# Block-sorted attention and an MLP on one core: more opening matmuls, instruction fetches in the planner, and K and V of three batches sorted on the whole array

## The chip, the cores and the metric

The kernel runs on one core of one Trainium2 chip. A core has five engines that run side by side: PE (TensorE, matrix multiplication, into the accumulators called PSUM), DVE (VectorE), ACT (ScalarE), POOL (GpSimd) and SP (SyncE, which here only issues DMAs). Each works through its own list of instructions in order, and they wait for each other by semaphores. DMA moves data between the chip's main memory and the on-chip memory (SBUF, 128 partitions). The metric is the device time of one execution in microseconds (us), lower is better; the time before is the median of three runs.

## The reference

Attention over blocks that are first mixed by a learned, normalised matrix, and then a two-layer MLP with a leaky activation. There are 4 batches, 8 heads, 768 rows of 64; 8 blocks of 96 rows per head.

```python
P = sort_net                                  # 4 x 8 x 8 x 8
for _ in range(5):
    P = P - np.max(P, axis=-1, keepdims=True)
    P = np.exp(P)
    P = P / (np.sum(P, axis=-1, keepdims=True) + 1e-09)
    P = P / (np.sum(P, axis=-2, keepdims=True) + 1e-09)
k_sorted = np.einsum('bhij,bhjcd->bhicd', P, k_b)      # k, v as 8 blocks of 96 rows
v_sorted = np.einsum('bhij,bhjcd->bhicd', P, v_b)
scores = scale * np.matmul(q_b, k_sb.transpose(0, 1, 2, 4, 3))   # inside each block
attn = softmax(scores)
x = np.matmul(attn, v_sb)                     # then to 3072 tokens x 512
h = x @ w_in                                  # 512 x 2048
g = np.maximum(h, 0.0) + alpha * np.minimum(h, 0.0)
out = g @ w_out                               # 2048 x 512
```

"Sorting" below is the product with P over the blocks.

## The kernel before

**A plan written out ahead.** The kernel first builds a graph of operations. Each operation (`G.add`) names its engine or engines, the instructions it issues, an estimated duration, what it reads and writes, and a priority (smaller is earlier). `schedule` fills all engines by list scheduling with these durations, `span` gives one operation's begin and end, `replay` runs the found order again with random extra durations, and `search` repeats the whole 1500 times with slightly changed priorities and keeps the order with the smallest end. `emit` then writes the order of each engine into the program, with semaphore waits. So the order on every engine is fixed before the kernel runs, and a change of an estimated duration changes the order. `fill` puts warm-up matmuls (L883) into gaps of PE up to the start of the MLP.

**Inputs.** POOL issues the loads of q, k, v and the weights, which are converted from float32 to bfloat16 on the way. q, k and v of a batch come as 128 partitions of 3072 elements (`load_q`, `load_kv`); a partition holds half a block, 48 rows. Later batches' loads are paced: they wait for a certain transpose of the attention (`paced`), so that they do not crowd out the transposes.

**Sort matrices.** `sinkhorn` makes P on DVE and ACT for all batches. `spread` widens it with small PE matmuls and builds on DVE one matrix per batch, `BDK`, of 128 x 128 with one 8 x 8 block per head and half; batch 0 at once, batches 1 to 3 after the first x tile is written.

**Sorting.** K of a batch is sorted in 6 units, V in 8 (`prep_k`, `prep_v`). A K unit is 16 matmuls of 64 x 64 (L540, in `pairs`): 8 columns groups, each as an upper and a lower half of the array. A V unit is 16 matmuls of 128 x 64 weights (L583), which write the upper and lower half of the output. V is first copied from its staging tile `VST` into `VD`, where each group of 48 columns is widened to 64 (`conv_v`); for batches 1 to 3 POOL does this, in 8 copies for each batch. `VD` holds a whole batch. The sorted units go from PSUM to `KT` and `VS` by ACT or DVE.

**Attention.** `attention(g)` runs for 32 groups (4 batches of 8 blocks): scores (L618, L621), the maximum on DVE (L627), exponentials on ACT (L654, L665), the product with V (L674), division on DVE (L681, L684). In batch 0 the scores are made a second time in transposed form (L633, L642), and the result is turned on PE (L699); in later batches SP issues DMA transposes of the exponentials (`ET<-Esb`) and of the result (`xT<-xq`).

**MLP.** `ffn1` (L721) multiplies tiles of x by `w_in`, ACT and DVE apply the activation (L731, L734) into `hT`, and `ffn2` (L760) multiplies by `w_out`. It runs in pieces of 2 or 4 groups, interleaved with the attention of later groups.

**The opening.** 70 small matmuls (`burst`, L785) keep PE busy from the start. Then come q's reordering (L540 on `QS`), the sort network, K and V of batch 0, two groups of attention and the first MLP step. Loads in order of issue on POOL: q, k, v of batch 0, `w_in` in four pieces of 512 columns, `w_out` in two, k of batch 1, q of batch 1, then v of batch 1 and k, v of batch 2.

Of the kernel before, what the change touches and what calls it, by code (L numbers as in the profile page):

```python
# [25 lines left out]
NE = 3  # L26
EPS = 1e-9
SEARCH = 1500

# [18 lines left out]
class _Op:  # L48
    __slots__ = ("eng", "fn", "dur", "prio", "deps", "dma", "idx", "pos", "inc", "start", "end",
                 "users", "left", "ready", "turn", "engs", "base")  # L50

    def __init__(self, eng, fn, dur, prio, dma, idx):
        self.eng, self.fn, self.dur, self.prio, self.dma, self.idx = eng, fn, dur, prio, dma, idx
        self.deps = set()
        self.turn = set()
        self.users = []
        self.inc = None
        self.engs = eng


class _Graph:
# [7 lines left out]
    def add(self, eng, fn, dur, r=(), w=(), prio=0.0, dma=None):  # L69
        op = _Op(eng, fn, dur, prio, dma, len(self.ops))  # L70
        if eng == ("pool",) and dma is None:
            w = list(w) + ["pool cores"]
# [19 lines left out]
    def span(self, op, e, at, free, loads, more=0.0):  # L92

        if op.dma is None:
            d = op.dur[e] if isinstance(op.dur, dict) else op.dur
            return at + d * (1 + more), at + d * (1 + more)
# [7 lines left out]
        return at + 1300, loads[1]  # L104

# [13 lines left out]
    def schedule(self):  # L119
# [17 lines left out]
        loads = [0.0, 0.0]  # L137
# [30 lines left out]
    def replay(self, seed):  # L168
# [5 lines left out]
        loads = [0.0, 0.0]  # L174
# [3 lines left out]
        last = max(op.end for op in self.ops)  # L178
        for op, (a, b) in zip(self.ops, was):
            op.start, op.end = a, b  # L180
        return last

    def search(self, n):
# [4 lines left out]
        for x in range(n):  # L188
            amp = rng.choice((0.1, 0.3, 1.0))
            for op, p in zip(self.ops, rank):  # L190
                op.prio = p + (rng.uniform(-amp, amp) if x and p > -47.5 and rng.random() < 0.1 else 0.0)
            cost = self.schedule()
            if best is None or cost < best + 1500:
                cost = (cost + self.replay(1) + self.replay(2)) / 3
# [95 lines left out]
def bass_sinkhorn_attn__then__act_prelu_kernel(  # L290
# [38 lines left out]
    dsel = sb("dsel", [128, 3, 8], F32)  # L329
    BDK = sb("BDK", [128, 4, 128], BF16)  # L330
    epst = sb("epst", [32, 8], F32)
# [7 lines left out]
    QS = [sb("QS0", [128, 3072], BF16)]  # L339
# [3 lines left out]
    VD = sb("VD", [128, 64, 64], BF16)  # L343
# [3 lines left out]
    Es0 = [sb("Es0%d" % n, [112, 800], BF16) for n in range(2)]  # L347
# [8 lines left out]
    outstg = [sb("outstg%d" % n, [128, DM], F32) for n in range(4)]  # L356
    dtmp = outstg[3]

# [28 lines left out]
    d_v = [dma_sem("v%d" % n) for n in range(7)]  # L387
# [8 lines left out]
    def load_q(b, prio):  # L396
        if b == 0:
            G.add(POOL, lambda e: e.dma_start(QS[0][:, :], AP(q.tensor, 0, [[3072, 128], [1, 3072]])),
# [30 lines left out]
    def load_v(b, prio):  # L429
        load_kv(VST, v, "VST", d_v, 9, b, prio)  # L430

    def consts():
# [7 lines left out]
        G.add(POOL, lambda e: e.memset(AP(VD, 48, [[4096, 128], [64, 64], [1, 16]]), 0.0), 900,  # L440
              w=["VD0"], prio=-95.5)
        for n in range(2):
            G.add(DVE, lambda e, n=n: e.memset(AP(Es0[n], 768, [[800, 112], [1, 32]]), 0.0), 100, w=[("Es0p", n)], prio=-88)
        for n in range(NE):
            G.add(DVE, lambda e, n=n: e.memset(AP(ET[n], 768, [[800, 128], [1, 32]]), 0.0), 100, w=[("ETp", n)], prio=-30)
# [13 lines left out]
        for n in range(NE):  # L459
# [4 lines left out]
              r=["identf"], w=["mkj"], prio=-70)  # L464
        G.add(DVE, lambda e: e.tensor_reduce(one0[:, :], AP(identf, 0, [[128, 112], [64, 2], [1, 48]]),
# [13 lines left out]
    def bc(t):  # L479
        return AP(t, 0, [[8, 32], [1, 8], [0, 8]])  # L480

# [25 lines left out]
    def spread(bs, prio):  # L507
        n = len(bs)

        def f(e):  # L510
# [4 lines left out]
        G.add(PE, f, 100 * n, r=["Pb", "selk"] + [("xT", 1)] * (bs[0] > 0), w=PSP, prio=prio)  # L515
        G.add(DVE, lambda e: e.tensor_tensor(
            out=AP(dtmp, 0, [[512, 128], [8, 8 * n], [1, 8]]),
            in0=AP(psYP, 512, [[1024, 128], [8, 8 * n], [1, 8]]),
            in1=AP(mkj, 0, [[8, 128], [0, 8 * n], [1, 8]]), op=AluOpType.mult), 150 + 70 * n,
            r=PSP + ["mkj"], w=["dtmp", ("out", 3)], prio=prio)  # L520
        G.add(DVE, lambda e: e.reduce_sum(AP(dsel, 0, [[24, 128], [1, 8 * n]]),
                                          AP(dtmp, 0, [[512, 128], [8, 8 * n], [1, 8]]),
                                          axis=AxisListType.X), 150 + 70 * n,
              r=["dtmp", ("out", 3)], w=["dsel"], prio=prio)
        for x, b in enumerate(bs):
            G.add(DVE, lambda e, x=x, b=b: e.tensor_tensor(
                out=AP(BDK, b * 128, [[512, 128], [16, 8], [2, 8], [1, 2]]),
                in0=AP(mkh, 0, [[16, 128], [2, 8], [0, 8], [1, 2]]),
                in1=AP(dsel, x * 8, [[24, 128], [0, 8], [1, 8], [0, 2]]), op=AluOpType.mult), 260,
                r=["dsel", "mkh"], w=[("BDK", b)], prio=prio)  # L530

    def pairs(src, n, u, mat, off_m, row_m, bank):
        t, off, row, keys = bank

        def f(e):
            inst = None
            for c in range(8):
                cc = 8 * u + c
                for hp in range(2):
                    inst = e.matmul(AP(t, hp * 64 * row + off + c * 64, [[row, 64], [1, 64]]),  # L540
                                    AP(src, hp * 64 * 3072 + cc * 64, [[3072, 64], [1, 64]]),
# [4 lines left out]
    def prep_q(u, prio, bank):  # L546
        t, off, row, keys = bank
        G.add(PE, pairs(QS[0], 0, u, identb, 0, 128, bank), 372, r=[("QS", 0), "identb"], w=keys, prio=prio)
        o = AP(QTz[0], 8 * u, [[6144, 128], [96, 32], [48, 2], [1, 8]])
        i = AP(t, off, [[row, 128], [2, 32], [1, 2], [64, 8]])  # L550
        G.add(EITHER, lambda e: copy(e, o, i), t_either(512), r=keys, w=[("Q0", u)], prio=prio)
# [374 lines left out]
```

## Time and profile before

| | before |
|---|---|
| median of 3 runs | 259.07 us (257.0 to 260.28) |
| the profiled execution | 259.23 us |
| its span, first to last instruction | 257.5 us |
| mean granted PE clock | 0.973 |
| warm-up matmuls L883 | 37, 11.6 us busy |
| MLP matmuls L721 to psH | 556, 97.0 us busy |
| MLP matmuls L760 to psYP | 306, 80.0 us busy |

The profile gives, for one execution, the busy time of each engine, groups of equal instructions by source line, the waits with what ended them, and a chain of work followed back from the last instruction. PE's matmuls are pipelined: the length of one matmul (200 to 400 ns) is its way through the array, while the next begins long before. What a group of matmuls costs PE is therefore the distance between its start and the start of the next group. PEld is the loading of weights, which runs beside the matmuls. "issue" as a releaser means that the engine waited for nothing the profile shows. A few records of matmuls are missing.

### The profile page before, as it was taken

Reading aid. Unit: us, or ns where it says so; the run is one execution under the profiler, and the core shown is the slowest. Engines: PE = TensorE matmul, PEld = TensorE weight load, DVE = VectorE, ACT = ScalarE, POOL = GpSimd, SP = SyncE. Lnnn points to the kernel's source line nnn. Section 1 sums busy time; section 2 is a strip of 40 time slices with the busy share of each in tenths; the row PEclk is TensorE's granted clock in tenths of the full one; section 3 lists DMA queues with packets and bytes.
Section 4 is the critical chain, followed back from the end, with each engine's and each line's share of the span. In section 5 each row is a group of like instructions: output and inputs, shape, how many; then the busy total and the mean of one; then the engine's idle time right before and its main releaser. Section 6 shows DMA issues by size and latency. Waiting matters only on the chain.

```text
span 257.5 us, 6566 instructions
## 1 busy us (share of the span) xinstructions
PE 238.7 (93%) x2721; PEld 147.2 (57%) x2752; DVE 166.2 (65%) x330; ACT 154.1 (60%) x419; POOL 61.4 (24%) x89
## 2 busy tenths in 40 slices
PE   7687799979999997989899999999999999999995
PEld 4355577767656564645565565555555565555544
DVE  5773577666676896756887667466477795655510
ACT  4473444555775976758856654857667775555511
POOL 8999000194493020867100000000000000000000
PEclk9997779988999999999999999999999999999999
DMA  5999999999299989999985961212537234201112
GB/s 100 214 203 203 190 217 165 215 173 196 66 89 197 142 128 158 174 179 178 138 141 129 162 136 59 44 45 75 118 93 97 47 95 113 71 5 40 76 44 83
DMA packets 77070, 32.17 MB, mean 125 GB/s; under 512 B 67808, under 2 KB 73200, under 8 KB 77040
## 3 DMA queue, kind: packets, MB, share of 16 engines
q0 software_dynamic: 25168, 13.63, 40.8%
q1 hardware_dynamic: 51872, 18.11, 38.5%
q8 instruction: 21, 0.34, 0.6%
q14 instruction: 9, 0.07, 0.1%
HBM read 27.28 MB, written 6.29 MB: 130 GB/s over the span
## 4 chain that ended last, share of the span: by engine, by line
PE 76%; DMA 8%; POOL 6%; DVE 3%; issue 3%; ACT 3%; POOLq 0%
PE psH L721 28%; PE psYP L760 25%; DMA ET<-Esb 8%; PE psYP L583 4%; PE psS L760 3%; PE psO L674 3%; PE psS L618 3%; PE psS L633 2%; PE psYP L540 2%; ACT Esb L654 1%; POOL QN L447 1%; PE psYP L883 1%; POOL w_in_bf L803 1%; PE psS L642 1%; PE psO L583 1%
## 5 line engine op out<-in xcount | busy, mean ns | idle before, releaser
L734 DVE SCALAR_TENSOR_TENSOR hT<-t,omaT,psH 128x384 bf16<-128x384 f32 (+1 forms) x139 | 77.6, 572 | 41.2 <-ACT t L731 39.7
L721 PE MATMUL psH<-xT,w_in_bf 128*128 128x384 bf16 (+1 forms) x556 | 97.0, 312 | 0.9 <-DVE hT L734 0.7
L731 ACT ACTIVATE t<-psH 128x384 f32<-128x384 f32 (+1 forms) x139 | 62.3, 465 | 42.5 <-PE psH L721 39.8
L760 PE MATMUL psYP<-w_out_bf,hT 128*128 128x512 bf16 x306 | 80.0, 382 | 2.9 <-issue 1.3
L721 PEld LDWEIGHTS psH<-xT,w_in_bf 128*128 128x128 bf16 x556 | 50.9, 98 | 33.9 <-DVE hT L734 5.9
L654 ACT ACTIVATE Esb<-psS,nf 96x96 bf16<-96x96 f32 x192 | 46.3, 344 | 1.5 <-DVE nf L627 1.3
L760 PEld LDWEIGHTS psYP<-w_out_bf,hT 128*128 128x128 bf16 x336 | 30.6, 98 | 27.9 <-issue 0.6
L373 POOL COPY VD<-VST 128x384 bf16<-128x384 bf16 x26 | 22.6, 869 | 33.8 <-DMA VST<-in_v_dram 25.7
L627 DVE TENSOR_REDUCE nf<-psS 96x8 f32<-96x768 f32 x24 | 22.7, 948 | 2.1 <-PE psS L618 1.9
L684 DVE TENSOR_TENSOR xq<-psO,rec 96x512 bf16<-96x512 f32 x31 | 21.3, 687 | 1.1
L402 POOL DMA_DIRECT2D QN<-in_q_dram x24 | 19.8, 845 | 2.3 <-DMA xT<-xq 1.8
L373 ACT ACTIVATE outstg<-psYP 128x512 f32<-128x512 f32 x15 | 9.0, 597 | 12.7 <-PE psYP L760 12.7
L583 PE MATMUL psYP<-BDK,VD 128*64 128x64 bf16 x416 | 12.1, 202 | 3.5 <-issue 2.0
L681 DVE RECIPROCAL rec<-psO 96x8 f32<-96x8 f32 x31 | 6.2, 201 | 13.2 <-PE psO L674 13.1
L373 ACT ACTIVATE VS<-psYP 112x512 bf16<-112x512 f32 x14 | 9.7, 690 | 7.6 <-PE psYP L583 7.2
L583 PEld LDWEIGHTS psYP<-BDK,VD 128*64 128x64 bf16 x416 | 9.1, 114 | 8.6 <-issue 4.2
L618 PEld LDWEIGHTS psS<-KT,QTz 128*96 128x96 bf16 x192 | 11.6, 124 | 3.2 <-ACT Esb L654 0.4
L373 ACT ACTIVATE KT<-psYP 128x512 bf16<-128x512 f32 x13 | 7.8, 597 | 9.5 <-PE psYP L540 9.5
L618 PE MATMUL psS<-KT,QTz 128*96 128x96 bf16 x192 | 12.8, 209 | 0.0
L674 PEld LDWEIGHTS psO<-VS,ET 112*128 112x128 bf16 x192 | 8.6, 98 | 6.4 <-DMA ET<-Esb 3.0
L883 PE MATMUL psYP<-identb 128*128 128x512 bf16 x37 | 11.6, 438 | 0.3 <-ACT identb L373 0.3
L674 PE MATMUL psO<-VS,ET 112*128 112x65 bf16 x192 | 9.9, 194 | 1.6 <-DMA ET<-Esb 1.6
(116 smaller groups left out, 183.3 us busy)
## 6 DMA issues: line engine op xcount, KB each, us to landing
out_dram<-outstg SPq DMA_DIRECT2D x23, 256.0 KB, 2.3
KS<-in_k_dram POOLq DMA_DIRECT2D x3, 768.0 KB, 30.0
VST<-in_v_dram POOLq DMA_DIRECT2D x3, 768.0 KB, 26.7
QN<-in_q_dram POOLq DMA_DIRECT2D x24, 96.0 KB, 6.5
w_in_bf<-in_moe_w_in_dram POOLq DMA_DIRECT2D x4, 512.0 KB, 17.2
w_out_bf<-in_moe_w_out_dram POOLq DMA_DIRECT2D x2, 1024.0 KB, 27.1
QS<-in_q_dram POOLq DMA_DIRECT2D x1, 768.0 KB, 7.1
VST<-in_v_dram POOLq DMA_DIRECT2D x4, 192.0 KB, 5.4
```

The lines of the kernel that those rows point to most:

```text
L373: return e.activation(o, i, ACTF.Copy) if e is nc.scalar else e.tensor_copy(o, i)
L402: G.add(POOL, lambda e, h=h: e.dma_start(AP(QN, h * 128 + (h // 4) * 64, [[6144, 128], [1024, 6], [1, 64]]), AP(q.tensor, b * HB + h * S * ...
L583: inst = e.matmul(AP(t, th * 64 * row + off + dd * 64, [[row, 64], [1, 64]]), AP(VD, (8 * u + dd) * 64, [[4096, 128], [1, 64]]), AP(BDK, b ...
L618: inst = e.matmul(o, AP(QTz[n], hp * 3072 + h4 * 768 + i * 96, [[6144, 128], [1, 96]]), AP(KT[n], (h4 * 8 + i) * bk, [[ld, 128], [64, 2], ...
L627: G.add(DVE, lambda e: e.tensor_reduce(AP(nx, 0, [[8, 96], [4, 2], [1, 4]]), AP(psX, 0, [[1024, 96], [512, 2], [96, 4], [1, 96]]), AxisLis ...
L654: inst = e.activation(AP(Esb[me], p * 128, [[1024, 96], [64, 2], [1, 48]]), AP(psX, (p // 4) * 512 + (p % 4) * 96, [[1024, 96], [48, 2], [ ...
L674: inst = e.matmul(AP(psZ, hp * 512 + h4 * 68, [[1024, 128], [1, 65]]), AP(ET[me] if far else Es0[m], pos(h4, hp) * 96, [[800, nk], [1, 128]]),
L684: G.add(DVE, lambda e: e.tensor_tensor(out=AP(xq[me], 0, [[512, 96], [256, 2], [64, 4], [1, 64]]), in0=AP(psZ, 0, [[1024, 96], [512, 2], [ ...
L721: inst = e.matmul(AP(pt, poff, [[1024, 128], [1, n]]), AP(w_in_bf, kt * DFF + ft * 128, [[KT_TILES * DFF, 128], [1, 128]]), AP(xT, kt * XR ...
L731: G.add(ACT, lambda e: e.activation(AP(t1[tb], 0, [[384, 128], [1, n]]), AP(pt, poff, [[1024, 128], [1, n]]), ACTF.Relu, scale=-1.0), t_ac ...
L734: G.add(DVE, lambda e: e.scalar_tensor_tensor(out=AP(hT, ft * RING + tok % RING, [[FT_TILES * RING, 128], [1, n]]), in0=AP(t1[tb], 0, [[38 ...
L760: inst = e.matmul(AP(bank[0], bank[1], [[1024, 128], [1, n]]), AP(hT, ft * RING + tok % RING, [[FT_TILES * RING, 128], [1, 128]]), AP(w_ou ...
```

## The change

- The opening burst has 140 matmuls instead of 70.
- The planner gets a model of PE's instruction fetches: a count of PE's instructions, with a mark every 256, and the next mark cannot be passed earlier than 6.2 us after the last one. `search` has a first phase of 500 rounds that minimises the sum of the ends of the first four x tiles, and then the 1500 rounds of before, which now vary only priorities above 0.
- K of batches 1 to 3: POOL copies each unit in two halves into a ring of three units (`KSz`), in which each group of 64 columns lies in a field of 128 whose other half is zero. A unit is then 8 matmuls with 128 x 128 weights instead of 16 with 64 x 64. The moving operand is a new compact matrix `BDM`.
- V of batches 1 to 3: loaded as two halves (first and second halves of blocks on different partitions), copied in two halves per unit into a ring of four units (`VDz`) in the same manner; for batch 1 the second halves may go to ACT or DVE, all others go to POOL. 8 matmuls per unit, with a matrix `BDV`.
- `spread` of batches 1 to 3 makes these two matrices per batch: six more matmuls and more DVE steps; there are three more masks. POOL zeroes the two rings once.
- `w_in` comes in four pieces of 128 rows instead of 512 columns, and each MLP step reads all four.
- Batch 0's `VD` and `QS` lie in the space of `hT`; `Es0` is replaced by `ET`; q's units of batch 0 are copied by ACT alone.

```diff
+FIRST = 500
+FETCH = 6200.0
+BURST = 140
...
+            if e == "pe":
+                return (self.fetched(op, at, d * (1 + more), loads[2]),) * 2
...
+    def fetched(self, op, at, d, f):
+
+        if f["fills"] and at > 5000:
+            f["n"] += 2 * int(max(at - f["end"], 0) * 0.9 / 215)
+        f["fills"] = f["fills"] and op.fills
+        n, last = 2 * op.mm, f["n"] + 2 * op.mm
+        while f["mark"] < last:
+            x = at + d * max(f["mark"] - f["n"], 0) / n
+            late = max(f["usable"] - x, 0.0)
+            at, x = at + late, x + late
+            f["usable"] = x + FETCH
+            f["mark"] += 256
+        f["n"], f["end"] = last, at + d
+        return at + d
...
-        for x in range(n):
+        for x in range(FIRST + n):
+            if x == FIRST:
+                best = None
+            lo, hi, part = (-47.5, 3.0, 0.2) if x < FIRST else (0.0, 99.0, 0.1)
...
+            if x < FIRST:
+                cost = sum(op.end for op in first)
...
+        n = 2 if b == 3 else 1
+        t = 3072 // n
+        for x in range(2 * n):
+            G.add(POOL, lambda e, th=x % 2, c=x // 2 * t: e.dma_start(
+                AP(VST[b % 2], th * 64 * 3072 + c, [[3072, 64], [1, t]]),
+                AP(v.tensor, b * HB + th * 3072 + c, [[6144, 64], [1, t]])), load_us / (2 * n),
...
+        G.add(POOL, lambda e: e.memset(zk[:, :], 0.0), 1500, w=[("KSz", u, hp) for u in range(3) for hp in range(2)],
+              prio=0.05)
...
+    def conv_k(b, u, prio):
+        n = b % 2
+        for hp in range(2):
+            G.add(POOL, lambda e, hp=hp: e.tensor_copy(
+                AP(KSz, hp * 64 * 3072 + u % 3 * 1024 + hp * 64, [[3072, 64], [128, 8], [1, 64]]),
+                AP(KS[n], hp * 64 * 3072 + 8 * u * 64, [[3072, 64], [64, 8], [1, 64]])), 900,
+                r=[("KS", n)] + [("KS", n, x) for x in range(4)], w=[("KSz", u % 3, hp)], prio=prio)
...
+            for c in range(8):
+                inst = e.matmul(AP(t, off + c * 64, [[row, 128], [1, 64]]),
+                                AP(KSz, (u % 3 * 8 + c) * 128, [[3072, 128], [1, 128]]),
+                                AP(BDM, b * 64, [[256, 128], [1, 64]]))
...
-        G.add(POOL if b or u % 3 == 2 else EITHER, lambda e: copy(e, o, i), {"act": 858, "dve": 540, "pool": 720},
-              r=[("VST", b % 2)] + [("VST", b % 2, x) for x in range(4)], w=[("VD", u)], prio=prio)
...
+        for th in range(2):
+            o2 = AP(VDz, th * 64 * VSL * 1024 + u % VSL * 1024 + th * 64, [[VSL * 1024, 64], [128, 8], [1, 48]])
+            i2 = AP(VST[b % 2], th * 64 * 3072 + 8 * u, [[3072, 64], [1, 8], [64, 48]])
+            G.add(EITHER if b == 1 and th else POOL, lambda e, o2=o2, i2=i2: copy(e, o2, i2),
+                  {"act": 858, "dve": 540, "pool": 830}, r=vst, w=[("VDz", u % VSL, th)], prio=prio)
...
+                if b:
+                    inst = e.matmul(AP(t, off + dd * 64, [[row, 128], [1, 64]]),
+                                    AP(VDz, (u % VSL * 8 + dd) * 128, [[VSL * 1024, 128], [1, 128]]),
+                                    AP(BDV, b * 64, [[256, 128], [1, 64]]))
+                    continue
...
-        for _ in range(70):
+        for _ in range(BURST):
...
-            AP(w_in_bf, p * 512, [[KT_TILES * DFF, 128], [DFF, KT_TILES], [1, 512]]),
-            AP(moe_w_in.tensor, p * 512, [[DFF, 128], [128 * DFF, KT_TILES], [1, 512]])),
+            AP(w_in_bf, p * DFF, [[KT_TILES * DFF, 128], [1, DFF]]),
+            AP(moe_w_in.tensor, p * 128 * DFF, [[DFF, 128], [1, DFF]])),
...
-            units = [(prep_k, b + 1, u) for u in range(6)]
+            units = [(conv_k, b + 1, u) for u in range(2)]
+            for u in range(6):
+                units += [(prep_k, b + 1, u)] + [(conv_k, b + 1, u + 2)] * (u < 4)
```

More of the change, by code (lines that the diff above doesn't have):

```diff
@@ L178, in replay @@
         last = max(op.end for op in self.ops)
+        self.ends = [op.end for op in self.ops]
         for op, (a, b) in zip(self.ops, was):
@@ L181, in replay, with search @@
         return last
-    def search(self, n):
+    def search(self, n, first):
         rng = random.Random(7)
@@ L508, in spread @@
         n = len(bs)
+        late = bs[0] > 0
+        rows = n * (1 + late)
         def f(e):
@@ L521, in spread @@
[L521 to L524, printed above, removed]
+            for x in range(n * late):
+                for hf in range(2):
+                    inst = e.matmul(AP(psYP, hf * 64 * 1024 + 512 + (n + x) * 64, [[1024, 64], [1, 64]]),
+                                    AP(selk, bs[x] * 128, [[512, 32], [2, 64]]), Pb[:, :])
```

161 lines of the change are left out of this document (116 added, 45 removed).

## The prediction

> **What bounds the kernel now.** I read the page's first part, then the stretches of the span, then the chain of waits.
>
> ```profile
> span 257.5 us, 6566 instructions
> PE 238.7 (93%) x2721; PEld 147.2 (57%) x2752; DVE 166.2 (65%) x330; ACT 154.1 (60%) x419; POOL 61.4 (24%) x89
> ...
> 0.00:32.20 32.20, 24.38 (x507) 16.37 (x507) 20.01 (x66) 15.90 (x30) 23.72 (x41) 0.89 1.04 182
> 32.20:60.00 27.80, 26.02 (x397) 19.66 (x397) 19.28 (x44) 14.18 (x34) 7.55 (x9) 0.88 1.42 195
> 60.00:130.00 70.00, 64.83 (x854) 40.66 (x863) 50.32 (x91) 50.25 (x151) 30.12 (x39) 1.00 1.22 146
> 130.00:245.00 115.00, 113.69 (x912) 64.64 (x927) 75.53 (x129) 71.69 (x202) 0.00 (x0) 1.00 0.40 86
> ```
>
> A row of a stretch gives its length, the busy time and instructions of PE, PEld, DVE, ACT and POOL, then the granted clock. Two regimes: up to 32.2 us, where the first MLP matmul starts, PE serves a chain of dependent steps; after it PE is the bound, idle 1.78, 5.17 and 1.31 us in the three later stretches. So a microsecond taken from PE's work after 32.2 is worth nearly one of the end, and one taken from the opening chain too, as all later PE work starts that much earlier. From 130 us POOL does nothing, and there is little idle time to win.
>
> The chain through the opening, and PE's and DVE's own steps around it (start, length, engine, line):
>
> ```profile
> 18.82 0.38 PE psYP L583 x11
> 19.20 2.03 issue
> 21.23 0.25 PE psYP L583 x4
> 21.48 0.75 PE psYP L883 x3
> ...
> 22.57 0.91 PE psS L633 x8
> ...
> 28.26 0.54 PE psYP L883
> ...
> 39.13 0.54 PE psS L633 x8
> ...
> 1.02 2.04 PE L785 MATMUL psS<-bz 128*32 128x32 bf16 x70 [1.02 <-DVE bz L780]
> ...
> 9.48 0.67 PE L540 MATMUL psS<-identb,QS 64*64 64x64 bf16 x32
> ...
> 14.88 0.44 PE L540 MATMUL psO<-BDK,KS 64*64 64x64 bf16 x16 [0.26 <-issue]
> ...
> 16.36 0.44 PE L540 MATMUL psH<-BDK,KS 64*64 64x64 bf16 x16
> ...
> 19.94 0.93 DVE L627 TENSOR_REDUCE nm<-psH 96x8 bf16<-96x768 f32 x1
> ...
> 32.21 1.04 PE L721 MATMUL psH<-xT,w_in_bf 128*128 128x192 bf16 x8
> ```
>
> Two things stand out. In the middle of one group of sorting matmuls PE stops for 2.03 us and waits for nothing that the profile shows. And the same eight L633 matmuls take 0.91 us at 22.57 and 0.54 at 39.13. The stretches say why:
>
> ```profile
> 14.88:19.30 4.42, 3.76 (x127) 2.65 (x127) 4.16 (x7) 4.06 (x8) 4.30 (x6) 1.00 1.23 208
> ...
> 18.86:22.27 3.41, 1.38 (x23) 0.68 (x25) 2.02 (x3) 1.67 (x3) 3.41 (x5) 1.00 1.23 203
> 22.27:25.68 3.41, 3.41 (x58) 3.02 (x60) 0.69 (x1) 0.96 (x2) 3.27 (x6) 0.53 1.24 204
> 25.68:29.10 3.42, 3.42 (x77) 2.60 (x71) 1.57 (x3) 2.03 (x3) 0.00 (x0) 0.50 1.15 173
> ```
>
> From the gap of 0.26 us before 14.88, which has no releaser either, PE had run 127 matmuls and 127 weight loads, 254 instructions; it went on at 21.23, 6.35 us after that gap. I read that as PE running out of delivered instructions: some 256 per 6.3 us. And the clock is granted at half right after a stretch in which PE was busy 1.38 of 3.41 us, the one with the stop, and stays there to about 29.
>
> **The opening, part by part.** Seventy more opening matmuls are 140 more PE instructions at the front, where PE only keeps warm: the 70 of before lie between 1.02 and 3.06 us, and 140 would end near 5.1, well ahead of the q matmuls. If instructions come in blocks of 256, every boundary falls 140 instructions, that is 70 matmuls, earlier in the work. The one that fell inside the third V unit moves back into the end of the K units, 6.3 us after a boundary in the last q matmuls near 10, thus due at about 16.3, while the last K unit starts at 16.36: no wait, or one of 0.1. The next is 128 matmuls on, some 60 past the old stop, due near 22.7, where PE would arrive near 22. So of 2.03 us I take 1.6 as won, leaving 0.4 for the boundary near 22; bounds 2.0 won and 2.0 lost (a second stop of that length). Late next is the maximum of the second score group, on DVE until 20.87, well inside the won time.
>
> In the Trainium skill, "Runtime: NRT & Kernel Launch", section "Instruction fetch mechanics", instructions are refilled in blocks of 256, which agrees with the 254 counted; it also holds that the fetch is hidden behind the sequencer's own pace, and the 2.03 us speak against that. By that section of the Trainium skill the first term would be zero, and the sum below 253.0.
>
> The clock: 21.48 to 28.26 are 6.8 us of mostly PE pieces at half clock. By the L633 pair, full clock makes it 0.54/0.91 = 0.59, so 2.8 us less. The half clock need not go altogether, since the waits of this stretch leave PE partly idle anyway; bounds 0 and 2.8, taken 2.2. What else lies below full clock from 32.2 to 60, at 0.88 on average, I leave as it is.
>
> The new search that orders the work up to the first four x tiles, and q's copies on ACT alone, I cost at nothing; the sort network on DVE still covers them. w_in now has to be there whole for the first MLP matmul:
>
> ```profile
> 4.34 3.00 POOL L803 DMA_DIRECT2D w_in_bf<-in_moe_w_in_dram  x4
> ...
> DMA to landing us min/median/max: 14.3/17.2/20.4
> ```
>
> The last is issued at about 6.6 and lands by 27.0 at the latest; the first MLP matmul would come at 32.2 − 3.8 = 28.4. Cover 1.4 us, cost zero; without that cover each microsecond of lateness costs one.
>
> **The sorting matmuls.** For batches 1 to 3 each of 6 K and 8 V units has 8 full-array matmuls instead of 16 small ones: 42 units. Prices are distances between starts of neighbours on PE:
>
> ```profile
> 128.15 0.44 PE L583 MATMUL psYP<-BDK,VD 128*64 128x64 bf16 x16
> 128.52 0.56 PE L618 MATMUL psS<-KT,QTz 128*96 128x96 bf16 x8
> ...
> 134.56 0.41 PE L674 MATMUL psO<-VS,ET 112*128 112x65 bf16 x8
> 134.80 1.47 PE L721 MATMUL psH<-xT,w_in_bf 128*128 128x384 bf16 x8
> ...
> 158.62 0.44 PE L540 MATMUL psYP<-BDK,KS 64*64 64x64 bf16 x16
> 159.00 1.04 PE L760 MATMUL psYP<-w_out_bf,hT 128*128 128x512 bf16 x4
> ```
>
> A V unit holds PE 0.37 us, a K unit 0.38. L674 has nearly the new shape (8 matmuls, 112 by 128 weights, 65 columns) and holds it 0.24. Saving 0.13 × 42 = 5.5 us, all in the regime where PE is the bound; bounds 0 (PE then waits instead) and 5.9. It also takes 336 matmuls, 672 instructions, out of the stream.
>
> **What POOL gets.** The longest waits and the copies:
>
> ```profile
> L373 POOL COPY VD<-VST x26: 829/849/1199, 17.6 to 111.1; 128x384 bf16<-128x384 bf16 x26
> L563 POOL COPY KT<-KT 128x512 bf16<-128x512 bf16 x1 | 0.7, 722 | 0.0
> ...
> 81.96 0.56 POOL L420 DMA_DIRECT2D VST<-in_v_dram  x1 [3.14 <-DMA ET<-Esb]
> 90.99 1.07 POOL L420 DMA_DIRECT2D VST<-in_v_dram  x2 [8.47 <-DMA ET<-Esb]
> 95.28 0.53 POOL L420 DMA_DIRECT2D KS<-in_k_dram  x1 [3.22 <-DMA ET<-Esb]
> 100.13 0.53 POOL L420 DMA_DIRECT2D VST<-in_v_dram  x1 [4.32 <-DMA xT<-xq]
> 103.66 1.05 POOL L420 DMA_DIRECT2D KS<-in_k_dram  x2 [3.00 <-DMA ET<-Esb]
> ```
>
> A copy works on half the partitions with as many elements in each, so I take V at 0.85 us a half and K at 0.72 (nearest row 128x512; bounds 0.36, if half the partitions cost half, and 1.20, the longest copy). Per batch: 16 × 0.85 + 12 × 0.72 = 22.2 us where 8 copies took 6.8. Three batches make 46 us more at most, 6.8 less if the eight second halves of batch 1 go to ACT or DVE; three memsets of 3584 elements in all, some 5 us at the pace of the 128x512 copy, come last in priority, and from 32.2 to 60 POOL is busy 7.55 of 27.80 us. Up to 130 us POOL is busy 61 us, so there is room in sum. But before, V was copied up to a whole batch ahead; now three K units and four V units are the lead. And POOL runs in order: behind its paced loads of batch 3 stand copies of batch 2, for them PE. I charge 1.0 us of new PE idle time; bounds −2.0, since the 5.17 us idle in 60–130 could also shrink, and +15 (a rival below).
>
> Does the copying slow DVE? "GPSIMD Engine Reference" of the Trainium skill, section "Specifications", has POOL's SBUF interface shared with VectorE, against this change. The trace shows the first row beside eight POOL copies, the second without any:
>
> ```profile
> L734 DVE SCALAR_TENSOR_TENSOR hT<-t,omaT,psH 128x384 bf16<-128x384 f32 x5 | 3.0, 609 | 1.2 <-ACT t L731 1.1
> ...
> L734 DVE SCALAR_TENSOR_TENSOR hT<-t,omaT,psH 128x384 bf16<-128x384 f32 x44 | 26.4, 611 | 13.8 <-ACT t L731 13.3
> ```
>
> No slowing of the main DVE step, so the term is nothing.
>
> The rest: six more matmuls and some eight small DVE steps, each below the 0.61 us of L734, in the second spread and the masks, and up to eight copies of batch 1 on ACT or DVE, both busy under 75% from 32 to 130 us. Charged 0.5; bounds 0 and 2.0.
>
> **The sum.** The profiled execution took 259.23 us, 1.7 outside its span; the median of the three is 259.07, 0.2 below, which I neglect. 259.23 − 1.6 − 2.2 − 5.5 + 1.0 + 0.5 = 251.4 us, 3.0% less.
>
> **Rivals.**
>
> *The opening stays.* The 2.03 us stop has another cause, or falls elsewhere, and the half clock with it. For: no row names the cause, and one boundary is still due in the same stretch. Against: 254 instructions and 6.35 us fit a block well. Time: 259.23 − 5.5 + 1.5 = 255.2. The 140 matmuls would not do what they are there for. Chance 0.17. It is also the case to which the Trainium skill's sentence on the hidden fetch leads.
>
> *POOL becomes the bound around batch 2's sorting.* Between 78 and 104 us POOL waits 22.1 us in order for transposes (the five waits above) and issues 3.7 us of loads. Batch 2's 28 copies of 22.2 us now have to fit there: 48 us of 26. If the waits are not used up by the copies that stand ahead of them, 22 us are over; the V ring hides 4 units × 1.7 = 6.8, and PE stands still for 15: 251.4 − 1.0 + 15 = 265.4, slower. It decides once more than about 14 us reach PE. Against it: a wait shrinks when POOL comes to it later, and some loads can stand behind the copies. Chance 0.14.
>
> *More than forecast.* Half of the 8.3 us of PE idle from 32 to 245 goes too, because x arrives earlier and PE has fewer small groups: 251.4 − 4.1 = 247.3. Chance 0.11.
>
> **The numbers.** The forecast has 0.58, with its own range of 247.5 to 255. Measurements of this kernel can tell about 2% from no change, that is 5.2 us: faster is below 253.9, slower above 264.2. Faster: 0.49 of the forecast's 0.58, 0.11 of the third rival, 0.01 of the first; 0.61. Slower: the second rival but for 0.02, plus 0.02 for bounds adding up; 0.14. The rest is 0.25. The range, 245.5 to 260, takes in the first and third rival and leaves out most of the second and 0.03 below.
>
> **What would show it.** Right: no issue wait of 2 us before the first MLP matmul; that matmul at 28 to 29 us; granted clock 1.00 from 20 to 28; 42 groups of eight sorting matmuls that hold PE 0.24 to 0.25 us each; PE idle between 32 and 245 us near 9. Wrong: POOL copies released late and PE waiting for KSz or VDz between 75 and 130 us; sorting units that still hold PE 0.37; the first MLP matmul waiting for w_in.

## The result and the profile after

The changed kernel takes 251.78 us (median of five runs, 249.6 to 253.86), the kernel before 258.08 us in the same comparison (257.0 to 260.28). The ratio is 0.9702, 95% interval 0.963 to 0.9775: about 3% faster. The forecast was 251.4, 3.0% less. Executions more than 1.5% above the shortest of their kernel, the profiled one below among them, count in the medians but not in the ratios, so the two can differ.

The profiled execution took 253.86 us, the longest of the five, so single waits in it are not all typical; E8 below has a second profile of the same kernel. Its first part, then its stretches (length, busy time and instructions of PE, PEld, DVE, ACT and POOL, granted clock, DMA share, GB/s), cut at the first MLP matmul, which now starts at 28.60:

```profile
span 251.9 us, 6183 instructions
...
PE 234.7 (93%) x2494; PEld 146.1 (58%) x2494; DVE 170.3 (68%) x340; ACT 156.1 (62%) x423; POOL 100.0 (40%) x146
```

```profile
0.00:28.60 28.60, 23.00 (x583) 16.13 (x583) 20.26 (x67) 16.25 (x31) 26.49 (x46) 1.00 0.95 179
28.60:60.00 31.40, 29.42 (x362) 22.16 (x356) 21.95 (x53) 16.82 (x39) 11.46 (x18) 0.84 1.36 193
60.00:130.00 70.00, 63.98 (x687) 40.29 (x686) 53.49 (x96) 52.40 (x155) 56.52 (x75) 1.00 1.19 151
130.00:245.00 115.00, 114.13 (x841) 64.30 (x838) 74.22 (x127) 69.69 (x199) 5.56 (x10) 1.00 0.37 86
```

The opening is 3.6 us shorter and runs at full clock throughout. PE is idle 1.98, 6.02 and 0.87 us in the later stretches, 8.87 in all, where the forecast had "near 9". POOL has gone from 61.4 to 100.0 us. But from 28.6 to 60 the clock is 0.84 on average. Three finer stretches of the same profile show where the low clock went:

```profile
18.86:22.27 3.41, 3.22 (x88) 2.14 (x83) 2.02 (x4) 1.82 (x4) 3.17 (x6) 1.00 1.06 214
22.00:28.60 6.60, 4.87 (x101) 3.63 (x93) 4.71 (x9) 3.28 (x5) 6.60 (x10) 1.00 1.09 181
28.60:34.00 5.40, 5.40 (x59) 4.03 (x54) 3.63 (x13) 1.69 (x4) 0.50 (x1) 0.68 1.22 200
```

From 18.86 to 22.27 PE was busy 1.38 us before and is busy 3.22 now: the stop is gone. No "issue" is among the waits of PE. The half clock now comes after 28.6, in the first MLP work.

From the timeline of PE (start, length, line, matmul, count): the first MLP matmul, then a K unit and a V unit, each with the group that follows it.

```profile
28.60 0.82 PE L854 MATMUL psH<-xT,w_in_bf 128*128 128x192 bf16 x4
...
45.65 0.39 PE L664 MATMUL psYP<-BDM,KSz 128*128 128x64 bf16 x8
45.88 0.49 PE L854 MATMUL psH<-xT,w_in_bf 128*128 128x192 bf16 x4
...
135.95 0.40 PE L705 MATMUL psYP<-BDV,VDz 128*128 128x64 bf16 x8
136.18 1.47 PE L854 MATMUL psH<-xT,w_in_bf 128*128 128x384 bf16 x8
```

Each unit holds PE 0.23 us, against 0.37 and 0.38 before. POOL's copies and its longest waits (copies: count, busy us, mean ns, idle before; waits: total us, times, longest):

```profile
L423 POOL COPY VDz<-VST 64x384 bf16<-64x384 bf16 x40 | 33.7, 842 | 13.6 <-PE psYP L705 11.5
L651 POOL COPY KSz<-KS 64x512 bf16<-64x512 bf16 x36 | 22.1, 614 | 36.6 <-PE psYP L664 21.0 <-DMA KS<-in_k_dram 13.8
```

```profile
POOL QN L452 <- DMA xT<-xq: 1.7, 2, 0.9
POOL KS L470 <- DMA xT<-xq: 0.9, 1, 0.9
```

POOL's paced loads wait for transposes 2.6 us in all; before it was 25.9, of which the five waits quoted in the prediction made 22.1. The 21.0 us in the second copy row are POOL waiting for PE to give a ring slot back, so POOL has time over. And in this execution PE never waits for `KSz` or `VDz`.

### The profile page after: what moved, and what is told of

Read it like the earlier page. It is cut to its first block, busy times and chain, and to the rows that moved or that the text cites. A ratio compares the mean times of both kernels' runs of the same rounds, so it can differ in the third digit from the quotient of the medians.

```text
span 251.9 us, 6183 instructions
## 1 busy us (share of the span) xinstructions
PE 234.7 (93%) x2494; PEld 146.1 (58%) x2494; DVE 170.3 (68%) x340; ACT 156.1 (62%) x423; POOL 100.0 (40%) x146
## 4 chain that ended last, share of the span: by engine, by line
PE 60%; DMA 25%; DVE 6%; ACT 5%; POOL 3%; issue 1%
PE psH L854 26%; PE psYP L893 23%; DMA VST<-in_v_dram 15%; DMA ET<-Esb 9%; PE psS L893 3%; PE psO L804 2%; PE psS L748 2%; DVE hT L867 2%; ACT Esb L784 2%; PE psYP L705 1%; ACT t L864 1%; DVE VDz L423 1%; PE psYP L664 1%; POOL w_in_bf L937 1%; DVE xq L815 1%; POOL w_out_bf L942 1%
## 5 line engine op out<-in xcount | busy, mean ns | idle before, releaser
L854 PE MATMUL psH<-xT,w_in_bf 128*128 128x384 bf16 (+1 forms) x556 | 98.8, 315 | 1.9 <-DVE hT L867 1.8
L893 PE MATMUL psYP<-w_out_bf,hT 128*128 128x512 bf16 x336 | 84.4, 381 | 1.2 <-DVE outstg L423 0.6
L423 POOL COPY VDz<-VST 64x384 bf16<-64x384 bf16 x40 | 33.7, 842 | 13.6 <-PE psYP L705 11.5
L651 POOL COPY KSz<-KS 64x512 bf16<-64x512 bf16 x36 | 22.1, 614 | 36.6 <-PE psYP L664 21.0
L804 PEld LDWEIGHTS psO<-VS,ET 112*128 112x128 bf16 x248 | 11.3, 99 | 7.8 <-DMA ET<-Esb 1.6
L804 PE MATMUL psO<-VS,ET 112*128 112x65 bf16 x248 | 12.9, 196 | 2.6 <-DMA ET<-Esb 2.6
L423 ACT ACTIVATE VS<-psYP 112x512 bf16<-112x512 f32 x16 | 11.0, 686 | 4.5 <-PE psYP L705 1.9
L1019 PE MATMUL psYP<-identb 128*128 128x512 bf16 x39 | 10.7, 383 | 0.0
L705 PE MATMUL psYP<-BDV,VDz 128*128 128x64 bf16 x192 | 9.6, 193 | 0.7 <-DVE VS L423 0.4
L705 PEld LDWEIGHTS psYP<-BDV,VDz 128*128 128x128 bf16 x192 | 8.0, 98 | 2.4 <-DVE VS L423 1.1
```

The source lines that it names most:

```text
L423: return e.activation(o, i, ACTF.Copy) if e is nc.scalar else e.tensor_copy(o, i)
L651: G.add(POOL, lambda e, hp=hp: e.tensor_copy(AP(KSz, hp * 64 * 3072 + u % 3 * 1024 + hp * 64, [[3072, 64], [128, 8], [1, 64]]), AP(KS[n], ...
L705: inst = e.matmul(AP(t, off + dd * 64, [[row, 128], [1, 64]]), AP(VDz, (u % VSL * 8 + dd) * 128, [[VSL * 1024, 128], [1, 128]]), AP(BDV, b ...
L804: inst = e.matmul(AP(psZ, hp * 512 + h4 * 68, [[1024, 128], [1, 65]]), AP(ET[me] if far else ET[m], pos(h4, hp) * 96, [[800, nk], [1, 128] ...
L854: inst = e.matmul(AP(pt, poff, [[1024, 128], [1, n]]), AP(w_in_bf, kt * DFF + ft * 128, [[KT_TILES * DFF, 128], [1, 128]]), AP(xT, kt * XR ...
L893: inst = e.matmul(AP(bank[0], bank[1], [[1024, 128], [1, n]]), AP(hT, ft * RING + tok % RING, [[FT_TILES * RING, 128], [1, 128]]), AP(w_ou ...
```

## The experiments

Ratios are to the kernel before, run on the same chip in the same comparison, with their 95% intervals.

**E1. The burst alone.** The kernel before with 140 opening matmuls; its plan stays as it is.

```diff
-        for _ in range(70):
+        for _ in range(140):
```

> The kernel before with 140 opening matmuls and nothing else; the planned order of every engine is the old one. If PE gets its instructions in blocks of 256 about 6.3 us apart, the stop of 2.03 us in the third V unit goes, a boundary some 60 matmuls later costs at most 0.7 us, the clock is granted in full from 20 to 28 us, the first MLP matmul comes at 28.5 to 30.5 us instead of 32.2, and the time falls by 2 to 3.5 us, ratio 0.986 to 0.993. If the stop has another cause (a DMA, a semaphore, a fixed moment), it stays in the same unit at 2 us and the time is that of before.

Measured: 0.990 (0.985 to 0.9951), 255.23 us; about 2.6 us. The chain of waits passes through the third V unit with no issue step, and the MLP starts 3.75 us earlier (timeline of PE, then stretches of E1):

```profile
28.46 1.46 PE L721 MATMUL psH<-xT,w_in_bf 128*128 128x192 bf16 x8
```

```profile
26.00:28.00 2.00, 1.08 (x16) 0.79 (x16) 1.17 (x3) 0.84 (x2) 0.00 (x0) 0.87 1.19 187
28.00:30.00 2.00, 1.90 (x19) 1.37 (x17) 1.79 (x5) 0.51 (x3) 0.00 (x0) 0.50 1.22 197
30.00:32.00 2.00, 2.00 (x21) 1.83 (x22) 1.12 (x5) 0.88 (x2) 0.00 (x0) 0.50 1.21 178
```

The stop goes as forecast, but a half-clock stretch opens near 27.5, right behind a stretch in which PE waits for single steps (1.08 of 2.00 us busy). As the plan is the same, every group of matmuls can be set beside its twin of before: E1 is 3.8 us ahead at 28, 2.8 at 49, 4.3 from 59 to 86, 4.1 at 102, and then, in this execution, it loses most of it in one place. E1, and below it before:

```profile
107.84 0.81 PE L721 MATMUL psH<-xT,w_in_bf 128*128 128x384 bf16 x4
111.58 0.42 PE L674 MATMUL psO<-VS,ET 112*128 112x65 bf16 x8 [2.93 <-DMA ET<-Esb]
...
116.88 1.03 PE L760 MATMUL psYP<-w_out_bf,hT 128*128 128x512 bf16 x4
```

```profile
111.70 0.81 PE L721 MATMUL psH<-xT,w_in_bf 128*128 128x384 bf16 x4
113.27 0.42 PE L674 MATMUL psO<-VS,ET 112*128 112x65 bf16 x8 [0.75 <-DMA ET<-Esb]
...
116.91 1.03 PE L760 MATMUL psYP<-w_out_bf,hT 128*128 128x512 bf16 x3
```

PE arrives 3.86 us earlier, waits 2.93 us for a DMA transpose instead of 0.75, comes out 1.69 ahead, and by 116.9 is 0.03 ahead, since the clock drops after the wait (0.63 on average from 114 to 117, where it was 1.00 before). At the end it is 1.2 us ahead. This execution took 257.99 us, well over E1's median, so the loss is not this large each time; it shows one way in which earliness is lost.

**E2. The next block.** The same loop with 198 matmuls, 128 more than before, that is 256 instructions with the weight loads. If blocks of 256 count, the boundary falls where it fell before.

```diff
-        for _ in range(70):
+        for _ in range(198):
```

> The kernel before with 198 opening matmuls: 128 more, which are 256 more PE instructions, so every boundary of 256 falls where it did with 70. Blocks of 256: the stop is back in the third V unit or just beside it, at 2 us or more, one block later in the stream (the boundaries of before at 8.6 and 14.9 us now come 6.3 us after one inside the burst, so they too are some 1.5 us later), the half clock after it is back, the first MLP matmul comes at 32 to 34.5 us, time equal to before or up to 2 us above. If more opening matmuls only help by keeping PE active, this is at least as good as with 140.

Measured: 1.0116 (1.0068 to 1.0164), 259.53 us. Timeline of PE and stretches of E2:

```profile
18.88 0.38 PE L583 MATMUL psYP<-BDK,VD 128*64 128x64 bf16 x12
21.42 0.32 PE L583 MATMUL psYP<-BDK,VD 128*64 128x64 bf16 x4 [2.16 <-issue]
...
33.55 1.46 PE L721 MATMUL psH<-xT,w_in_bf 128*128 128x192 bf16 x8
```

```profile
22.00:28.00 6.00, 6.00 (x101) 4.58 (x101) 1.43 (x3) 2.45 (x4) 3.62 (x6) 0.50 1.23 199
28.00:34.00 6.00, 4.99 (x59) 3.46 (x58) 3.33 (x7) 1.99 (x4) 0.00 (x0) 0.50 1.23 202
```

The stop is back in the same unit with 2.16 us, where it had 2.03, and so is the half clock. Seventy more matmuls remove it and 128 more restore it: what counts is the position in blocks of 256 instructions. A longer burst as such is worth nothing. The MLP starts 1.3 us later than before, and the time is up by about 3.0 us, more than the 2 that were expected at most.

**E3. The opening alone, with a new plan.** The changed kernel with K and V of batches 1 to 3 sorted as before: `VD`, the pairs of small matmuls, one copy per V unit, no rings. One of its lines:

```diff
-        G.add(PE, f, 250, r=[("KSz", u % 3, hp) for hp in range(2)] + [("BDM", b)], w=keys, prio=prio)
+        G.add(PE, pairs(KS[n], 0, u, BDK, b * 128, 512, bank), 372, r=ks + [("BDK", b)], w=keys, prio=prio)
```

> The changed kernel with K and V of batches 1 to 3 sorted as before (16 small matmuls for each unit, V copied whole by POOL, K not copied, one sort matrix, V loaded in one piece); opening, planner and w_in as changed. By the sum of the prediction the sorting gives 5.5 us less 1.5 of new waits, so this is 4 us slower than the changed kernel and 3 to 4 us faster than before: ratio 0.983 to 0.990, about 255.5. If the whole gain is the opening's: 0.970, 252. If it is the sorting's: 1.0, 258.

Measured: 0.9863 (0.9734 to 0.9993), 254.24 us. The first MLP matmul starts at 28.42. PE has two issue stops, 0.56 us up to 16.33 and 0.85 us up to 22.72. Against the changed kernel the new sorting is worth 0.9863 − 0.9702 = 0.016, some 4.1 us; with these two intervals anything from 0.3 to 8 us is possible.

**E4. The changed kernel with 70 opening matmuls,** planned anew for them.

```diff
-BURST = 140
+BURST = 70
```

> The changed kernel with 70 opening matmuls; the planner counts fetches and orders the work anew. If the position of the boundaries matters and the planner can only partly dodge it, the first MLP matmul comes 0.8 to 2 us later than 28.6 and the time is 1 to 2 us above the changed kernel, ratio 0.974 to 0.980. If the planner's knowledge is enough by itself: the same 28.6 and 0.970. If the number of opening matmuls does it all, a stop of 2 us and half the clock, 3.5 us above: 0.984.

Measured: 0.9783 (0.9684 to 0.9881), 251.65 us. PE has issue stops of 0.50 and 1.17 us, which end at 14.96 and 21.32, near the 14.88 and 21.23 of before; the MLP starts at 30.41. The new order makes the long stop shorter and avoids neither. The loss against the changed kernel can't be told from zero.

**E5. The sorting alone.** The changed kernel with the old opening: 70 matmuls, no count of fetches, the old search, `w_in` by columns. Two of its edits:

```diff
-BURST = 140
+BURST = 70
...
-                return (self.fetched(op, at, d * (1 + more), loads[2]),) * 2
+                return at + d * (1 + more), at + d * (1 + more)
```

> The changed kernel with the opening of before: 70 opening matmuls, no count of fetches in the planner, the old search, w_in by columns. What is left is the sorting on the whole array with its POOL copies. The sum of the prediction has 5.5 us less for PE and 1.5 of new waits: 4 us below before, 254 to 255, ratio 0.982 to 0.988; the stop of 2 us in the third V unit and the first MLP matmul near 32 are back. If the copies through POOL cost what PE saves: 1.0. If the two parts help each other (fewer PE instructions, fewer fetches): the same ratio as the whole change, 0.970.

Measured: 0.9724 (0.9666 to 0.9782), 250.19 us: no slower than the whole change, which was not expected. The long stop did not come back: with this plan PE comes to the boundary at 20.10 us, not at 19.20, and waits only 0.20 us there (timeline of PE in E5):

```profile
20.29 0.35 PE L702 MATMUL psO<-BDK,hT 128*64 128x64 bf16 x10 [0.20 <-issue]
...
26.13 0.35 PE L796 MATMUL psO<-VS,ET 112*128 112x65 bf16 x6 [0.62 <-issue]
...
31.30 0.84 PE L846 MATMUL psH<-xT,w_in_bf 128*128 128x192 bf16 x4
```

0.82 us of stops in all. Still the MLP starts 2.7 us later than in the changed kernel, and no cost of this shows in the time.

**E6. V of batch 1 on POOL alone.** In the changed kernel ACT waits in order for V of batch 1 to land, with an exponential behind the copies, and PE for that. Timeline of ACT, then of PE:

```profile
46.51 0.86 ACT L423 ACTIVATE VDz<-VST 64x384 bf16<-64x384 bf16 x1 [1.24 <-DMA VST<-in_v_dram]
...
47.73 0.86 ACT L423 ACTIVATE VDz<-VST 64x384 bf16<-64x384 bf16 x1
48.60 0.81 ACT L795 ACTIVATE ET<-psS 112x768 bf16<-112x768 f32 x1
```

```profile
49.46 0.56 PE L751 MATMUL psS<-KT,QTz 64*96 64x96 bf16 x8 [1.45 <-ACT ET L795]
```

```diff
-            G.add(EITHER if b == 1 and th else POOL, lambda e, o2=o2, i2=i2: copy(e, o2, i2),
+            G.add(POOL, lambda e, o2=o2, i2=i2: copy(e, o2, i2),
```

> The changed kernel with all V copies of batch 1 on POOL; the second halves no longer go to ACT and DVE. In the changed kernel ACT waited 1.24 us for V's DMA at 46.5 us with an activation of the MLP and an exponential queued behind it, PE then stood for 1.45 us and had half its clock for some 6 us. If that wait is a real cost of the change, it goes here, and the time is 1.5 to 3 us less: ratio 0.958 to 0.966. If POOL is the tighter place (8 more copies of 0.84 us between 51 and 70 us), V of batch 1 is sorted later, and the time is 1 to 3 us more: 0.974 to 0.982.

Measured: 0.9731 (0.9668 to 0.9794), 252.98 us. The wait for ACT is gone and the clock from 28.6 to 60 is 0.95, not 0.84; but PE is idle 8.92 us from 60 to 130, where it was 6.02 (stretches, then waits of PE, in E6):

```profile
60.00:130.00 70.00, 61.08 (x635) 37.20 (x634) 51.48 (x91) 46.57 (x144) 57.52 (x77) 0.98 1.28 154
```

```profile
PE psO L804 <- DMA ET<-Esb: 3.8, 4, 2.6
PE psYP L705 <- POOL VDz L423: 1.7, 3, 0.7
```

Neither range that was expected came: the wait is real, but the ratio is that of the changed kernel (E8). In this execution, a long one of 255.41 us, the time returns as waits for a transpose and for POOL.

**E7. Another seed** for the search of the changed kernel: how much of a difference is the plan's luck?

```diff
-        rng = random.Random(7)
+        rng = random.Random(11)
```

> The changed kernel with another seed for the planner's search; the work is the same, only the order differs. It measures how far a plan alone moves the time. If plans of one model are worth the same: 0.965 to 0.976. A larger distance would mean that the small differences between the other runs can't be told from the draw of a plan.

Measured: 0.9759 (0.9707 to 0.9811), 251.47 us. The difference from E8 is 0.003 and lies within the intervals, so differences of half a per cent between two plans say nothing of the edit. This plan has an issue stop of 1.07 us up to 22.62 and starts the MLP at 30.19: with the same edits, whether a stop is left depends on the order that the search finds.

**E8. The changed kernel once more,** in the same comparison as E5 to E7.

> The changed kernel once more, unaltered, beside the three that follow on the same chip. Ratio 0.963 to 0.978 as before; in the profile the first MLP matmul at 28.6 us and, if ACT's wait for V of batch 1 is a fixed part of the plan, PE idle for 1 to 2 us between 46 and 51 us on an exponential of ACT.

Measured: 0.9729 (0.9682 to 0.9775), 250.53 us; the profiled span is 248.6. PE's wait for ACT is there again, with 1.4 us, and so is the low clock, 0.89 from 28.6 to 60. No issue wait is among PE's; the MLP starts at 29.01, and PE is idle 1.59, 5.53 and 0.00 us in the three stretches from 28.6 to 245, 7.1 in all.

**E9. E5 with 140 opening matmuls,** no other edit.

```diff
-BURST = 70
+BURST = 140
```

> The kernel with the new sorting and the old opening, with 140 opening matmuls instead of 70 and the same order. With 70 it had no stop of 2 us left (gaps of 0.20 and 0.62 us), because its order reaches the boundaries later. If the 140 matmuls act only through that stop, they have nothing to win here: the same ratio as without them, 0.968 to 0.976, first MLP matmul 30.5 to 31.5 us. If they act by themselves, another 1% as in the kernel of before: 0.960 to 0.965.

Measured: 0.9735 (0.9666 to 0.9805), 250.4 us; the MLP starts at 29.74, earlier than expected. Where no long stop is left, no gain from the burst shows.

**E10. Each sorting matmul twice.** E5 with every matmul of the 42 units issued two times, in the same order on every engine; K's units likewise.

```diff
             for dd in range(8):
                 if b:
+                  for _ in range(2):
                     inst = e.matmul(AP(t, off + dd * 64, [[row, 128], [1, 64]]),
                                     AP(VDz, (u % VSL * 8 + dd) * 128, [[VSL * 1024, 128], [1, 128]]),
                                     AP(BDV, b * 64, [[256, 128], [1, 64]]))
-                    continue
+                  continue
```

> The kernel with the new sorting and the old opening, in which each matmul of the sorting of batches 1 to 3 is issued twice (the second writes the same result over the first); the order of all engines is the same. PE gets 42 times eight matmuls more, at 0.24 us a group 10.1 us. If PE is the bound from the first MLP matmul on, as the prediction has it, the end moves by 9 to 10.5 us: ratio 1.007 to 1.014. If the sorting lies half in time that PE waits through anyway, 5 us: 0.992.

Measured: 1.0115 (1.0053 to 1.0177), 259.54 us, 0.039 or 10.1 us over E5, give or take 2.2 by the two intervals. Timeline of PE in E10:

```profile
79.70 0.63 PE L699 MATMUL psYP<-BDV,VDz 128*128 128x64 bf16 x16
80.17 1.46 PE L848 MATMUL psH<-xT,w_in_bf 128*128 128x384 bf16 x8
```

A doubled unit holds PE 0.47 us, 0.24 more, and 42 × 0.24 = 10.1. As far as the intervals can tell, all of it reaches the end: what these units cost PE is what they cost the kernel, and the price of a unit is what the distance between neighbours says.

**E11. More work for POOL.** E5, in which each K copy of batches 2 and 3 is preceded by the same copy into a spare tile.

```diff
+    QS0d = sb("QS0d", [128, 512], BF16)
...
-            G.add(POOL, lambda e, hp=hp: e.tensor_copy(
+            G.add(POOL, lambda e, hp=hp: [e.tensor_copy(AP(QS0d, hp * 64 * 512, [[512, 64], [64, 8], [1, 64]]), AP(KS[n], hp * 64 * 3072 + 8 * u * 64, [[3072, 64], [64, 8], [1, 64]])) for _ in range(b > 1)] and None or e.tensor_copy(
                 AP(KSz, hp * 64 * 3072 + u % 3 * 1024 + hp * 64, [[3072, 64], [128, 8], [1, 64]]),
```

> The kernel with the new sorting and the old opening, in which POOL makes each K copy of batches 2 and 3 once more, into a spare tile, before the real one: 24 copies of about 0.61 us, 14.7 us more for POOL, 7.3 of them in batch 2's stretch from 60 to 110 us. Order of all engines the same. If POOL has room there (it was busy 57 of 70 us from 60 to 130), the time rises by less than 1.5 us: ratio 0.972 to 0.978. If POOL is what batch 2's sorting waits for, most of the 7.3 us arrives at the end: 0.990 to 1.0.

Measured: 0.9814 (0.9756 to 0.9871), 251.78 us, 0.009 or 2.3 us over E5; the intervals overlap. Copies of POOL, and the longest wait of PE, in E11:

```profile
L644 POOL COPY QS0d<-KS 64x512 bf16<-64x512 bf16 x24 | 14.6, 609 | 18.3 <-PE psYP L657 16.9
```

```profile
PE psYP L657 <- POOL KSz L644: 2.1, 2, 1.2
```

In E5 no wait of PE for `KSz` is listed. Of 14.6 us more on POOL some 2 reach the end, give or take 2: POOL has slack around batches 2 and 3, but not without end.

**E12. A wider search.** In the changed kernel the second phase may vary the opening's priorities too.

```diff
-            lo, hi, part = (-47.5, 3.0, 0.2) if x < FIRST else (0.0, 99.0, 0.1)
+            lo, hi, part = (-47.5, 3.0, 0.2) if x < FIRST else (-47.5, 99.0, 0.1)
```

> The changed kernel whose last 1500 rounds of the search may again move every priority above -47.5, as before the change, and not only those above 0. If the order up to the first four x tiles is worth its separate phase, the first MLP matmul comes later than 28.6 to 29.0 us and the time is equal or up to 2 us more: 0.971 to 0.980. If the early opening is bought with a worse middle (ACT waiting for V of batch 1), the whole search finds a better one: 0.960 to 0.968.

Measured: 0.9774 (0.9711 to 0.9838), 250.96 us, no better; the MLP starts at 29.30.

## Why the prediction was right, step by step

**The cause of the stop** was read rightly: E1 and E2 show by moving the boundary alone that the stop goes with the count of instructions; that PE waits there for their delivery is the reading that fits, and no row names it. The Trainium skill's sentence that the fetch is hidden ("Runtime: NRT & Kernel Launch", section "Instruction fetch mechanics") does not hold for these small matmuls; its blocks of 256 do. The two boundaries forecast at 16.3 and near 22 cost nothing that shows in E1 (no issue wait on PE); 0.4 us had been kept for them. They are there all the same: E3 stops up to 16.33 and 22.72, E7 up to 22.62. That the changed kernel has no stop at all is thus in part the luck of its plan.

**The opening's two terms, −1.6 and −2.2,** came out as events and not as time. The first MLP matmul starts at 28.60, forecast 28.4; the clock is 1.00 up to there. Alone, however, the two are worth 2.6 us (E1; 1.3 to 3.9 by the interval) instead of 3.8. How they divide can be estimated from the executions that the ratios count: time × (1 − mean granted clock) is what half clock takes, if PE had work all the while, and the rest is the time at full clock.

| kernel (runs) | taken by half clock, us | the rest, us |
|---|---|---|
| before (28) | 6.3 | 250.7 |
| E1, burst alone (7) | 3.5 | 251.2 |
| E5, sorting alone (5) | 2.9 | 247.1 |
| changed kernel and E8 (9) | 2.8 | 247.9 |

By this account the burst's gain is the clock: 2.8 us, near the upper bound given for that term, where 2.2 was taken. The 1.6 of the stop is the term that was mis-sized: in the rest, E1 has nothing left of it (+0.5, give or take 1). The step that failed is the rule that all PE work after the opening starts as much earlier and keeps it. Later work hangs on transfers too, and E1's trace shows one such place, the 2.93 us at 111.58.

**The sorting, −5.5, with +1.0 and +0.5 for what it brings,** that is −4.0, was right in size: −4.1 from E1 to E5 in the table (0.990 to 0.9724 in the ratios, 4.5 us), 4.1 from E3 to the changed kernel (0.3 to 8). The price per unit was right (0.23 for 0.24), and E10 shows that PE passes it on in full, to within 2.2 us. PE's idle time was right too (8.87 us, 7.1 in E8, for "near 9"), though its make-up was not: none of it in the profile after is for POOL. The K copies were cheaper than taken, 0.614 us for 0.72, the V copies as taken, 0.842 for 0.85; POOL gained 38.6 us, where 46 less 6.8, and some 5 for the memsets, were counted. The 0.5 for extra work on ACT and DVE was costed by length, not by order: an ACT copy that waits for a DMA holds the exponential behind it, and PE with it, 1.45 us. E6 gains nothing from taking this away.

**Why the parts don't add up.** E1 has 0.010 and E5 0.0276 by themselves; the sum of 0.0376 is more than the 0.0298 of the whole change, or the 0.0271 of E8. The intervals together are about 0.01, so this excess is only at the edge of what can be told; but E5 beside E8, in one comparison, shows no gain of the opening's edits on top of the new sorting, to within about 2 us. That the forecast's total came out so closely, with 3.8 us of it for the opening, is therefore partly luck. Part of the reason is shown: E5's plan had already escaped the long stop, and the half clock that followed it. Setting the stretches up to 60 us side by side, E8 and then E5:

```profile
29.00:60.00 31.00, 29.42 (x397) 22.58 (x391) 23.41 (x56) 18.25 (x42) 11.79 (x18) 0.89 1.37 196
```

```profile
31.30:60.00 28.70, 27.68 (x385) 21.57 (x384) 22.27 (x55) 19.11 (x44) 12.39 (x18) 0.96 1.38 195
```

Busy time × clock is 26.2 us in E8 and 26.6 in E5. E8 begins the MLP 2.3 us earlier and has done no more by 60 us; the lead went into half clock and into the wait for ACT. Each is one execution, and the times leave room for a difference of one to two us either way. The chain of work that ended last fits this. In the profile of E8, as in the one after, it does not run through the opening's matmuls up to 46 us but through the load of V of batch 1 (start, length):

```profile
9.29 36.57 DMA VST<-in_v_dram
```

ACT's copy waits for this load, and PE for the exponential behind the copy. What PE wins ahead of that point is then not on the chain. In E5 and E7 the chain runs through the opening instead, with issue stops of 0.62 and 1.07 us in it.

**The rivals.** "The opening stays" is refuted by E1 and E2. "POOL becomes the bound" is refuted for the change by its own waits, which shrank from 25.9 to 2.6 us as POOL came to them later, which is the argument that the prediction had against it; in E11, with 14.6 us more, PE begins to wait. "More than forecast" did not come: 8.87 us of idle time is not half of 8.3. The fetch count and the two-phase search, costed at nothing, show no worth that these runs can tell (E5, E9, E12).

**Open:** whether the landing of K and V of batch 1 bounds the stretch from 28 to 60 us; the chain above points at V, but loading in another order was not tried. How the 7 us of E5 would divide if its plan had kept the long stop is open too. No version measured is clearly faster than the changed kernel; E5 equals it with a simpler planner.

## What to carry to other kernels

Where an engine stops for nothing the profile shows, count its instructions since the last such gap: if the stops are a fixed count apart, shifting the count by half a block and by a whole one tells in two runs whether the count is the cause. An earlier start can be worth less than its size when transfers, or an engine that waits in order for one, stand further on; work on the busiest engine counted in full here (E10). Before crediting an edit inside a searched plan, run a second seed and the parts alone: here the same edits gave one plan without a stop and one with 1.07 us of it, and the parts did not add up.

## What the runs showed of the hardware

About half of the scatter of these times goes with the clock: over the 123 executions on record, each set against the mean of its kernel, time and time × (1 − clock) have a correlation of 0.69, whose square is 0.48. The mean granted clock of an execution lies within 0.001 of a few values (0.993, 0.986, 0.980, 0.973, 0.967, seldom 0.960 and 0.954). In its first comparison the changed kernel took 249.6 us at 0.993, 249.99 to 251.81 at 0.986, and 253.86 at 0.980; in E8 the two highest values make no difference (250.12 to 250.89 us at either). A step of 0.0067 in 250 us is 1.7 us, that is what some 3.4 us at half clock take. In the profiles of before, after, E1, E2, E5 and E8, half clock begins behind a stretch in which PE had waited: PE was busy 1.38 of 3.41 us there in the kernel before, 1.78 of 3.41 in the changed kernel from 46.33, and 1.82 of 3.41 in E5 from 25.87.

Where two issue stops follow each other in the opening, PE runs 127 matmuls and 127 weight loads between them, in five kernels alike, and their ends lie 5.8 to 6.4 us apart: 6.35 before, 5.86 in E2, 6.39 in E3, 6.36 in E4, 5.84 in E5.

A copy on POOL does not get cheaper with fewer partitions: 64 x 384 into `VDz` takes 842 ns, and the 128 x 384 copies into `VD` took 869 before. For K, 64 x 512 takes 614 ns; the one copy of 128 x 512 (`KT`) takes 609 in the profile after and 722 in the one before. Splitting a copy by partitions, as the rings need, costs about twice the time.
